# Quarter loads of the expert weights, output weights two units ahead in two buffers, and half of the single slots' second product in float32, in an attention, mixture-of-experts and gated-unit kernel

## The chip, the cores and the metric

The kernel runs as one program on 1 core of one Trainium2 chip. The metric is device time in microseconds (us). The engines are named as the profile names them: PE (TensorE, matmuls; PEld is its weight load), DVE (VectorE), ACT (ScalarE), POOL (GpSimd) and SP (SyncE, which here only issues DMAs). L12 is line 12 of the kernel before; the changed kernel has line numbers of its own.

## The reference

Three layers follow one another on 4608 tokens of width 512.

```python
kv = np.einsum('bhsd,bhse->bhde', k, v)          # 8 batches, 8 heads, 576 tokens, head size 64
out = np.einsum('bhsd,bhde->bhse', q, kv)
rms = np.sqrt(np.mean(out * out, axis=-1, keepdims=True) + 1e-06)
x = out / rms * g_norm                           # then as (4608, 512)

logits = x @ w_gate + modality_bias[modality_id] # 8 experts, one is chosen per token
e_idx = np.argmax(logits, axis=1)
gate_w = softmax(logits)[e_idx]
y[mask] = gate_w[mask] * (np.maximum(x[mask] @ w1[e], 0.0) @ w2[e])   # w1 512x1024, w2 1024x512

gate = 1.0 / (1.0 + np.exp(-(y @ w_gate)))       # the gated unit: w_gate, w_val 512x1536, w_out 1536x512
out = gate * (y @ w_val) @ w_out
```

## The kernel before, in words

**Attention and routing** fill the first 155 us or so: the keys' and values' products, the queries' turns and products in float32 (L296), then the ranks of the tokens within their experts.

**The expert stage** walks through 22 items that are always there and 4 spare ones behind a branch. Items 0 to 17 are pairs (two tiles of 128 tokens of one expert), items 18 to 21 are single slots (one tile each). Item t has four steps, j = 0 to 3, each with 256 of the 1024 hidden columns. A step (loop in `run`) does: the first product into `ph` (`emit_B`), the nonlinearity (`emit_h`), the second product of the step before into `py` (`emit_D`), and for single slots a turn of the hidden tile through PE (`emit_T`, tiles `hs`, `htp`). Products are split: each float32 operand is cut into a rounded part and a rest (`w1h`, `w1l` and so on, `split_w`, L738 on ACT and L739 on DVE), and three matmuls in float32r stand for one in float32.

The raw weights of item t lie in `w1r[t % 2]` and `w2r[t % 2]`, two buffers of 2 MiB for each matrix. (Buffer 0 of both is the tile `half` in the trace.) The kernel loads them two items ahead, a whole matrix per DMA, on SP (`load_w`, L699): w1 of item t+2 at step j = 2 of item t, w2 at j = 3, when the last quarter of the old contents has been split. The load is conditional: if the expert is that of item t, nothing is moved.

**Beside the expert stage** the weights of the gated unit, stored as doubles, are turned into float32 (`Decode`), and in the last four items the first rows of the expert output are read back, weighted and turned (`later`, `flip0`). A first unit's products (`gv_first`) follow the last step, then the last `emit_D` and `emit_y`, then every engine loads the count of used slots (L962) and branches (L963) round the spare items.

**The gated stage** has 60 units s, five blocks of 12; block 0 has units 0 to 11. In block 0 a unit is `glu_plain`: 12 matmuls of 128x512 for the gate product, 12 for the value product, and `out_step`: 12 for the output product of the unit before (L1109 to L1111). Between the products `prepare(s, spot)` is called at spots 0, 1, 6, 7, 2, 5, 4, 3, in this order. It sets the order of each engine's work: at spot 0 SP loads the next rows of weights, the next raw double weights and, in units 2 to 5, two `yr` tiles of the next block; spot 6 loads the output weights `wo` of the next unit into one buffer (`load_raw`, L554); spot 5 has POOL fetch gate values by index (`number`), spot 2 weights `yr` with them on ACT (`weigh`), spot 4 makes `wos`, `gh`, `gl` ready for the next output product (`ready_o`, L1088 to L1094) and turns `yr` on PE (L578); spot 3 decodes one late unit of weights and stores it (`decode_late2`, L148 to L152 and L1149 to L1159). SP takes all its DMAs in program order, and each instruction there that has to wait holds what is behind it.

In later blocks a unit is `glu_unit`, seven products of 6 matmuls and two output products. `YPLAN` says at which unit and spot which sum or split of the next block's inputs is made on ACT and DVE.

Of the kernel before, what the change touches and what calls it, by code (L numbers as in the profile page):

```python
# [82 lines left out]
def attention_moe_glu_kernel(  # L83
# [466 lines left out]
    raw_o = {}  # L550
# [127 lines left out]
    with ExitStack() as st:  # L678
# [9 lines left out]
        def load_w(t, which):  # L688
            if t >= end:
                return  # L690
            if which == 0:
                regs[t] = (nc.sync.value_load(est[0:1, t:t + 1], min_val=0, max_val=E - 1),
                           nc.sync.value_load(est[0:1, NITEM + t:NITEM + t + 1], min_val=0, max_val=1) if t < NSURE else None)
            if t >= NSURE:
                return
            e, new = regs[t]
            src, dst = (w1, w1r) if which == 0 else (w2, w2r)
            src = src[bass.ds(e, 1), :, :].rearrange("o (c p) f -> p (o c) f", p=128)
            nc.sync.dma_start(out=dst[t % 2], in_=src, cond=new, cond_hint=False)  # L699

        def load_piece(t, j, which):
            e = regs[t][0]
            p = dec.tile([128, 1024], F32, tag="d_raw", name="d_raw", bufs=4)
            if which == 0:
                src = w1[bass.ds(e, 1), :, j * 256:j * 256 + 256]
            else:
                src = w2[bass.ds(e, 1), j * 256:j * 256 + 256, :]
            p = p.rearrange("p (c f) -> p c f", f=src.shape[2])
            nc.sync.dma_start(out=p, in_=src.rearrange("o (c p) f -> p (o c) f", p=128))
            return p  # L710
# [12 lines left out]

        def split_w(t, j, which):
# [3 lines left out]
            raw, dst = ((w1r, w1s), (w2r, w2s))[which]  # L728
            nm = f"w{which + 1}"
            shape = [128, KC, 256] if which == 0 else [128, 2, DM]  # L730
            if t >= NSURE:
                src = load_piece(t, j, which)
            elif which == 0:
                src = raw[t % 2][:, :, j * 256:j * 256 + 256]
            else:
                src = raw[t % 2][:, 2 * j:2 * j + 2, :]
# [58 lines left out]
        def emit_T(t, j):  # L795
# [11 lines left out]
        def emit_D(t, j):  # L807
# [92 lines left out]
        def gv_first():  # L900
# [3 lines left out]
            glu_plain(lambda k: wt_first[k // 2][:, k % 2], y_of0, bank, tmp, lambda h: gm0, lambda p: None)  # L904

        def run(lo, hi):
# [10 lines left out]
            for which in range(2):  # L917
                for t in range(lo, lo + ahead):
                    load_w(t, which)
# [6 lines left out]
            for s, (t, j) in enumerate(steps):  # L926
# [5 lines left out]
                nt, nj = steps[s + 1] if s + 1 < len(steps) else (end, 0)  # L932
                split_w(nt, nj, 0)
# [21 lines left out]
            if sure:  # L955
                gv_first()
            emit_D(*steps[-1])
            emit_y(hi - 1)

        end = 0  # L960
        run(0, NSURE)
        used = nc.values_load(est[0:1, 2 * NITEM:2 * NITEM + 1], min_val=0, max_val=NSLOT)  # L962
        with tc.If(used > NSURE + NPAIR):  # L963
# [4 lines left out]
    with ExitStack() as st:  # L968
# [21 lines left out]
        gms = {(0, 0): gm0}  # L990
        split_o, split_g, acc = {}, {}, {}
# [279 lines left out]
```

## Time and profile before

| | |
|---|---|
| median of 3 runs | 1556.83 us (1555.05 to 1560.03) |
| the profiled execution | 1559.3 us |
| its span, first to last instruction | 1557.5 us |
| mean granted PE clock | 0.968 of full |
| PE busy | 1452.1 us (93%) |
| DVE, ACT, POOL busy | 919.9, 644.6, 229.3 us |
| mean DMA rate over the span | 229 GB/s |

The span lies 1.8 us below the profiled execution's own time. Busy shares are averages over stages that differ: the attention's first 155 us, the expert stage to about 660 us, block 0 of the gated stage to about 807 us, and the later blocks. PEclk of 1.00 is the clock of 2.4 GHz, 0.5 would be 1.2 GHz throughout.

### The profile page before, as it was taken

To read this page: it belongs to the slowest core of one execution; us is meant where nothing else is said; L and a number is where in the kernel's file an instruction comes from. 1 tells how busy PE (TensorE), PEld (TensorE's weight loads), DVE (VectorE), ACT (ScalarE), POOL (GpSimd) and SP (SyncE) were. 2 spreads that over 40 slices of the span, in tenths; PEclk is the share of its full clock that TensorE was granted. 3 is DMA by queue.
4 is the path that set the end of the run, shared out by engine and by line. 5 is a ranking of instruction groups with operands and counts; after the bars stand their busy time and mean duration, and the time that the engine had idled before them with its cause. 6 is when DMAs were issued, how large, how long until landed. Compare 5 with 4: busy or idle time off the path is not lost.

```text
span 1557.5 us, 22220 instructions
## 1 busy us (share of the span) xinstructions
PE 1452.1 (93%) x8649; PEld 1242.1 (80%) x8649; DVE 919.9 (59%) x1416; ACT 644.6 (41%) x1011; POOL 229.3 (15%) x302
## 2 busy tenths in 40 slices
PE   6993899999999998877789999999999999999997
PEld 5983799999999997655578887888888888888886
DVE  2568687887887886634576667434463346534341
ACT  3656455555555556723333334222232233212121
POOL 1121221232232122002001100102010020101011
PEclk9997899999999999988899999999999999999999
DMA  9976877857875747557578664656465655555444
GB/s 297 318 263 245 217 248 272 293 176 273 294 274 186 273 154 275 191 178 251 192 258 297 248 243 188 243 191 246 173 225 200 237 197 216 201 198 208 191 165 152
DMA packets 121950, 356.24 MB, mean 229 GB/s; under 512 B 18289, under 2 KB 39025, under 8 KB 114673
## 3 DMA queue, kind: packets, MB, share of 16 engines
q1 hardware_dynamic: 107632, 318.16, 57.7%
q0 software_dynamic: 11488, 36.27, 6.5%
q8 instruction: 70, 1.15, 0.3%
q10 hardware_dynamic: 2720, 0.35, 0.2%
q14 instruction: 40, 0.32, 0.1%
HBM read 311.27 MB, written 68.63 MB: 244 GB/s over the span
## 4 chain that ended last, share of the span: by engine, by line
PE 82%; issue 5%; DMA 5%; DVE 4%; ACT 2%; POOL 1%; SPq 0%; POOLq 0%; another core or an unknown queue 0%; ACTq 0%; DVEq 0%
PE gv L641 10%; PE gv L643 10%; PE gv L642 10%; PE ac L1109 6%; PE ac L1111 6%; PE ac L1110 6%; PE py L817 5%; PE py L816 5%; PE py L818 5%; PE ph L779 4%; PE ph L778 4%; PE ph L777 4%; PE kv L259 2%; PE ops L296 2%; DMA wo<-w_d 1%
## 5 line engine op out<-in xcount | busy, mean ns | idle before, releaser
L1109 PE MATMUL ac<-wos,gh 128*128 128x512 f32 x432 | 175.6, 406 | 28.0 <-ACT gh L1093 28.0
L1111 PE MATMUL ac<-wos,gl 128*128 128x512 f32 x432 | 175.1, 405 | 0.2
L1110 PE MATMUL ac<-wos,gh 128*128 128x512 f32 x432 | 174.3, 403 | 0.0
L645 DVE TENSOR_TENSOR gm<-u,gv 128x512 f32<-128x512 f32 x96 | 65.9, 686 | 173.9 <-PE gv L643 172.9
L777 PE MATMUL ph<-xh,w1h 128*128 128x256 f32 x576 | 166.8, 290 | 0.8 <-ACT xh L760 0.8
L779 PE MATMUL ph<-xl,w1h 128*128 128x256 f32 x576 | 164.0, 285 | 0.0
L778 PE MATMUL ph<-xh,w1l 128*128 128x256 f32 x576 | 163.8, 284 | 0.0
L665 ACT ACTIVATE s<-gv 128x512 f32<-128x512 f32 x48 | 28.8, 600 | 264.5 <-issue 207.6
L816 PE MATMUL py<-w2h,hh 128*128 128x512 f32 x320 | 126.6, 396 | 4.6 <-ACT hh L803 4.4
L817 PE MATMUL py<-w2l,hh 128*128 128x512 f32 x320 | 126.6, 396 | 0.8 <-DVE w2l L739 0.8
L818 PE MATMUL py<-w2h,hl 128*128 128x512 f32 x320 | 125.4, 392 | 0.0
L1109 PEld LDWEIGHTS ac<-wos,gh 128*128 128x128 f32 x432 | 84.6, 196 | 49.3 <-ACT gh L1093 32.1
L641 PE MATMUL gv<-half,wt 128*128 128x512 f32 x288 | 113.3, 394 | 1.9 <-DMA wt<-wt_d 1.9
L777 PEld LDWEIGHTS ph<-xh,w1h 128*128 128x128 f32 x576 | 111.2, 193 | 2.5 <-ACT xh L760 1.2
L643 PE MATMUL gv<-half,wt 128*128 128x512 f32 x288 | 112.4, 390 | 0.0
L778 PEld LDWEIGHTS ph<-xh,w1l 128*128 128x128 f32 x576 | 111.4, 193 | 1.4
L642 PE MATMUL gv<-half,wt 128*128 128x512 f32 x288 | 112.1, 389 | 0.0
L779 PEld LDWEIGHTS ph<-xl,w1h 128*128 128x128 f32 x576 | 111.1, 193 | 0.3 <-DVE xl L761 0.3
L1120 POOL DMA_INDIRECT out_dram<-ot,to x36 | 37.2, 1034 | 463.7 <-DVE ot L1115 191.8
L645 DVE TENSOR_TENSOR s<-u,gv 128x512 f32<-128x512 f32 x48 | 33.0, 687 | 119.7 <-PE gv L643 119.7
L1111 PEld LDWEIGHTS ac<-wos,gl 128*128 128x128 f32 x432 | 84.7, 196 | 21.6 <-DVE gl L1094 3.3
L1110 PEld LDWEIGHTS ac<-wos,gh 128*128 128x128 f32 x432 | 84.5, 196 | 18.2
(268 smaller groups left out, 3341.8 us busy)
## 6 DMA issues: line engine op xcount, KB each, us to landing
wt<-wt_d SPq DMA_DIRECT2D x36, 1792.0 KB, 7.5
half<-in_moe_w_dram SPq DMA_DIRECT2D x24, 2048.0 KB, 9.4
wos<-wo_d SPq DMA_DIRECT2D x96, 512.0 KB, 8.2
w1r<-in_moe_w_dram SPq DMA_DIRECT2D x11, 2048.0 KB, 9.2
w2r<-in_moe_w_dram SPq DMA_DIRECT2D x11, 2048.0 KB, 10.9
rows<-w_d SPq DMA_DIRECT2D x24, 512.0 KB, 7.3
wt_d<-wt SPq DMA_DIRECT2D x12, 1024.0 KB, 5.2
kt<-in_k_dram SPq DMA_DIRECT2D x8, 1152.0 KB, 8.9
```

Source lines behind the costliest of these rows:

```text
L641: nc.tensor.matmul(out=o, lhsT=wh, rhs=yh[:, c, :], start=first and c == 0, stop=False, skip_group_check=True)
L642: nc.tensor.matmul(out=o, lhsT=wh, rhs=yl[:, c, :], start=False, stop=False, skip_group_check=True)
L643: nc.tensor.matmul(out=o, lhsT=wl, rhs=yh[:, c, :], start=False, stop=last and c == 1, skip_group_check=True)
L777: nc.tensor.matmul(out=o, lhsT=bh[:, c, cs], rhs=hi[:, c, 0:n], start=(c == 0), stop=False)
L778: nc.tensor.matmul(out=o, lhsT=bl[:, c, cs], rhs=hi[:, c, 0:n], start=False, stop=False)
L779: nc.tensor.matmul(out=o, lhsT=bh[:, c, cs], rhs=lo[:, c, 0:n], start=False, stop=(c == KC - 1))
L816: nc.tensor.matmul(out=o, lhsT=hi[:, f, cs], rhs=bh[:, f, :], start=first, stop=False)
L817: nc.tensor.matmul(out=o, lhsT=hi[:, f, cs], rhs=bl[:, f, :], start=False, stop=False)
L818: nc.tensor.matmul(out=o, lhsT=lo[:, f, cs], rhs=bh[:, f, :], start=False, stop=last)
L1109: nc.tensor.matmul(out=o, lhsT=gh[:, cs], rhs=wh, start=(k == 0), stop=False)
L1110: nc.tensor.matmul(out=o, lhsT=gh[:, cs], rhs=wl, start=False, stop=False)
L1111: nc.tensor.matmul(out=o, lhsT=gl[:, cs], rhs=wh, start=False, stop=(k == NJ - 1))
```

## The change

Six edits.

1. `load_w` loads a quarter of a matrix (512 KiB) instead of a whole one, still on SP and conditional, for each step: the quarter of w1 of item t+2 as soon as the same quarter of item t has been split, the quarter of w2 likewise. A w1 quarter is read in rows of 1 KB, where the whole matrix had rows of 4 KB; w2 rows are 2 KB as before. `read_item` reads an item's expert and condition.
2. In single slots the second product of steps j = 1 and 3 is made in float32 from the raw weights and the unsplit hidden tile (`plain`): no split of w2 there (L738, L739), no rest of the hidden tile, and one matmul in place of three. The w2 quarter's load then waits for that product.
3. `gv_first` takes the last `emit_D` and `emit_y` between its two products, and the count is loaded ahead of it, so the branch follows the value product.
4. `wo` has a second buffer in the gated stage's pool; `load_raw` moves from spot 6 of unit s, for unit s+1, to spot 0 of unit s, for unit s+2, ahead of the rows.
5. `load_wt` loads in two pieces, the first of which holds the weights of the first product. Some tiles of the gated stage are named early, which places them elsewhere in memory.
6. `YPLAN` for blocks from 1 on spreads the steps over other spots.

```diff
     def load_raw(s, k):
-        raw_o[s, 0] = y0p.tile([128, DM], F32, tag="wo", name="wo", bufs=1)
+        raw_o[s, 0] = (y0p if k % 2 == 0 else late_pool[0]).tile([128, DM], F32, tag="wo", name="wo", bufs=1)
...
-            nc.sync.dma_start(out=dst[t % 2], in_=src, cond=new, cond_hint=False)
...
+        def load_w(t, j, which):
+            if t < min(end, NSURE):
+                e, new = regs[t]
+                nc.sync.dma_start(out=part(t, j, which), in_=source(e, j, which), cond=new, cond_hint=False)
...
+        def plain(t, j, which=1):
+            return t >= NPAIR and which == 1 and j % 2 == 1
...
+            if plain(t, j, which):
+                dst[t, j] = (src, None)
+                return
...
+            if plain(t, j):
+                h = ws.tile([128, 256], F32, tag="hs", name="hs").rearrange("p (f k) -> p f k", f=2)
+                nc.scalar.activation(out=h, in_=ps, func=ACTF.Copy)
+                hT_t[t, j] = (h, None)
+                return
...
+                    if lo is None:
+                        nc.tensor.matmul(out=o, lhsT=hi[:, f, cs], rhs=bh[:, f, :], start=first, stop=last)
+                        continue
...
                 split_w(nt, nj, 0)
-                if j == NJ1 - 2:
-                    load_w(t + ahead, 0)
+                if nj == 0:
+                    read_item(nt + ahead)
+                load_w(nt + ahead, nj, 0)
                 emit_h(t, j)
                 split_w(t, j, 1)
-                if j == NJ1 - 1:
-                    load_w(t + ahead, 1)
+                if not plain(t, j):
+                    load_w(t + ahead, j, 1)
...
                     emit_D(*steps[s - 1])
+                    if plain(*steps[s - 1]):
+                        load_w(steps[s - 1][0] + ahead, steps[s - 1][1], 1)
...
+            count.append(nc.values_load(est[0:1, 2 * NITEM:2 * NITEM + 1], min_val=0, max_val=NSLOT))
+            gv_first(last)
...
-                 {(10, 1): "cd", (10, 7): "ea", (10, 4): "f", (11, 1): "i", (11, 6): "g", (11, 7): "k", (11, 5): "bj", (11, 2): "h"}]
+                 {(10, 5): "c", (10, 2): "d", (10, 4): "e", (10, 3): "af", (11, 7): "i", (11, 5): "g", (11, 2): "k", (11, 4): "b", (11, 3): "jh"}]
...
-                nc.sync.dma_start(out=wts[s % 2][:, 0:n].bitcast(F32), in_=wt_d[s % NJ][:, 0:n])
+                for lo, hi in ((0, 1), (1, n)):
+                    nc.sync.dma_start(out=wts[s % 2][:, lo:hi].bitcast(F32), in_=wt_d[s % NJ][:, lo:hi])
...
             if spot == 0:
                 load_wt(s + 1)
+                if s + 2 <= NJ:
+                    load_raw(s + 2, s + 1)
                 load_rows(s + 2)
```

SP in one unit of block 0, before. `w_d<-w2r` is the store of the decoded weights, `rows` the next weight rows, `w2r<-in_moe_w` the next raw double weights, `wo` the output weights of the next unit:

```order
L150 DMA w_d_74<-w2r_8538 512x1x128
L1037 DMA rows_2065<-w_d_73 128x1024
L1144 DMA w2r_8538<-in_moe_w_out_dram 128x1024
L1129 DMA yr<-y_d 128x528 x2
L554 DMA wo<-w_d_73 128x512
L1062 DMA wt_d_80<-wt_7631 128x1536
L1090 DMA wo_d_91<-wos 128x1024
```

The same unit in the changed kernel:

```order
L150 DMA w_d_74<-w2r_8517 512x1x128
L554 DMA wo<-w_d_73 128x512
L1069 DMA rows_2065<-w_d_73 128x1024
L1175 DMA w2r_8517<-in_moe_w_out_dram 128x1024
L1160 DMA yr<-y_d 128x528 x2
L1095 DMA wt_d_80<-wt_7697 128x1536
L1121 DMA wo_d_91<-wos 128x1024
```

The `wo` load stands four issues earlier, and it is now the load for the unit after the next one; the store of the decoded weights is still ahead of all loads.

SP in the single slots, before, around the loads for item 20 (`half` is buffer 0):

```order
L699 DMA half_1706<-in_moe_w_dram 128x4x1024
L894 DMA rows_2065<-w_d_72 128x1024
L894 DMA rows_2066<-w_d_72 128x1024
L699 ISA
L699 DMA half_1706<-in_moe_w_dram 128x8x512
```

In the changed kernel quarters for item 20 stand even ahead of the first read of the expert output (`d_raw<-y_d`), and the rest is spread over the steps:

```order
L708 DMA half_1706<-in_moe_w_dram 128x4x256
L708 ISA
L708 DMA half_1706<-in_moe_w_dram 128x2x512
L880 DMA d_raw<-y_d 128x512
L881 DMA oid<-y_d 128x1
```

What was two DMAs of 2 MiB has become eight of 512 KiB; the first quarter of each matrix is issued three steps earlier than the whole was.

PE at the end of the expert stage, before: the value product of `gv_first` (`xtp`), the last second product (`py`), the count and the branch:

```order
L616 MATMUL xtp<-half_7565,d_raw 128x512
L617 MATMUL xtp<-half_7565,d_raw 128x512
L816 MATMUL py_7603<-w2h,hh 128x512
L817 MATMUL py_7603<-w2l,hh 128x512
L818 MATMUL py_7603<-w2h,hl 128x512
L816 MATMUL py_7603<-w2h,hh 128x512
L817 MATMUL py_7603<-w2l,hh 128x512
L818 MATMUL py_7603<-w2h,hl 128x512
L962 TENSOR_LOAD est
L963 COMPARE_AND_BRANCH
```

In the changed kernel, from the end of the gate product (`ph`) to the value product's first rows:

```order
L616 MATMUL ph<-half_7637,d_raw 128x512
L617 MATMUL ph<-half_7637,d_raw 128x512
L828 MATMUL py_7671<-w2r_2072,hs 128x512 x2
L615 MATMUL xtp<-half_7637,d_raw 128x512
L616 MATMUL xtp<-half_7637,d_raw 128x512
```

The last second product, two float32 matmuls on the raw weights in place of six, now lies between the two products; the count stands ahead of both, and the branch behind the value product.

## Rows read from the trace of the kernel before

**Rows 1.** Stretches of 40 us: engine busy us (instructions), granted clock, DMA share, GB/s

```profile
200.00:240.00 40.00, 40.00 (x261) 36.45 (x260) 31.64 (x39) 22.53 (x30) 7.75 (x9) 1.00 0.80 272
...
600.00:640.00 40.00, 31.86 (x181) 26.74 (x179) 27.48 (x32) 28.56 (x47) 9.11 (x10) 0.91 0.85 310
...
720.00:760.00 40.00, 31.70 (x116) 24.51 (x117) 19.91 (x31) 16.98 (x30) 4.98 (x8) 0.83 0.57 199
...
920.00:960.00 40.00, 37.47 (x159) 30.15 (x158) 30.55 (x45) 16.33 (x25) 0.00 (x0) 0.96 0.52 195
```

**Rows 2.** Waits from 655 to 812 us: engine line <- released by: total us, times, longest

```profile
ACT wos L1088 <- DMA wo<-w_d: 74.0, 10, 9.4
...
PE ac L1109 <- ACT gh L1093: 28.0, 9, 5.9
```

**Rows 3.** The chain that ended last, 700 to 815 us: start, us, what

```profile
742.81 0.32 SPq L152
...
744.67 5.99 DMA wo<-w_d
```

**Rows 4.** PE in order of time, in two units of the first block: start, us, what

```profile
736.68 0.50 PE L1109 MATMUL ac<-wos,gh 128*128 128x512 f32 x1 [2.29 <-ACT gh L1093]
...
744.30 1.03 PE L578 MATMUL tr<-ident,yr 128*128 128x128 f32 x8
...
751.94 0.60 PE L1109 MATMUL ac<-wos,gh 128*128 128x512 f32 x1 [3.85 <-ACT gh L1093]
```

**Rows 5.** PE at the end of the single slots, the branch, the first block's start

```profile
652.75 0.38 PE L801 MATMUL htp<-ident,hs 128*128 128x128 f32 x2
...
662.05 0.47 PE L615 MATMUL gv<-half,wt 128*128 128x512 f32 x1 [2.02 <-PEq L963]
...
669.14 0.50 PE L1109 MATMUL ac<-wos,gh 128*128 128x512 f32 x1 [2.83 <-ACT gh L1093]
...
673.93 0.39 PE L615 MATMUL gv<-half,wt 128*128 128x512 f32 x1
...
676.66 0.39 PE L615 MATMUL gv<-half,wt 128*128 128x512 f32 x1
```

**Rows 6.** DMA from 700 to 760 us, all queues together

```profile
DMA packets 5287, 13.18 MB, mean 220 GB/s; under 512 B 673, under 2 KB 1704, under 8 KB 5284
```

**Rows 7.** As rows 1, a stretch at the start of the second block

```profile
800.00:840.00 40.00, 38.06 (x168) 31.14 (x168) 29.87 (x52) 14.85 (x26) 7.48 (x11) 1.00 0.91 331
```

**Rows 8.** SyncE's DMA issues from 719 to 752 us

```profile
728.49 0.87 SPq L1129 DMA_DIRECT2D yr<-y_d  x2
```

**Rows 9.** POOL, the same stretch

```profile
734.13 0.18 POOL L566 COPY oid<-yr 128x1 int32<-128x1 int32 x1 [11.82 <-DMA yr<-y_d]
```

**Rows 10.** PE in order of time, 590 to 610 us, in the single slots

```profile
591.57 0.38 PE L801 MATMUL htp<-ident,hs 128*128 128x128 f32 x2
...
595.06 0.38 PE L801 MATMUL htp<-ident,hs 128*128 128x128 f32 x2
...
598.19 0.38 PE L801 MATMUL htp<-ident,hs 128*128 128x128 f32 x2
```

**Rows 11.** PE later in the single slots

```profile
625.61 0.56 PE L816 MATMUL py<-w2h,hh 128*128 128x512 f32 x1 [4.37 <-ACT hh L803]
...
640.75 0.66 PE L578 MATMUL xtp<-ident,d_raw 128*128 128x128 f32 x4 [1.03 <-DVE hl L804]
```

**Rows 12.** The chain that ended last, 598 to 700 us

```profile
606.15 17.57 DMA half<-in_moe_w_dram
```

**Rows 13.** The chain that ended last, 0 to 60 us, float32 matmuls of the attention

```profile
31.46 0.98 PE ops L296 x8
```

**Rows 14.** ACT at the branch

```profile
667.94 0.63 ACT L1088 ACTIVATE wos<-wo 128x512 fp32r<-128x512 f32 x1 [7.23 <-DMA y_d<-y,sidx]
```

**Rows 15.** PE at the start of the second block

```profile
806.93 0.50 PE L641 MATMUL gv<-half,wt 128*128 128x512 f32 x1 [1.94 <-DMA wt<-wt_d]
```

**Rows 16.** PE late in the second block

```profile
942.52 0.50 PE L641 MATMUL gv<-w2r,wt 128*128 128x512 f32 x1 [2.14 <-DVE u L645]
```

More of the change, by code (lines that the diff above doesn't have):

```diff
@@ L686, in attention_moe_glu_kernel, with read_item, part, source @@
         NJ1 = F1 // 256
[L688 to L691, printed above, removed]
+        def read_item(t):
+            if t < end:
                 regs[t] = (nc.sync.value_load(est[0:1, t:t + 1], min_val=0, max_val=E - 1),
                            nc.sync.value_load(est[0:1, NITEM + t:NITEM + t + 1], min_val=0, max_val=1) if t < NSURE else None)
[L694 to L698, printed above, removed]
-            nc.sync.dma_start(out=dst[t % 2], in_=src, cond=new, cond_hint=False)
-        def load_piece(t, j, which):
-            e = regs[t][0]
-            p = dec.tile([128, 1024], F32, tag="d_raw", name="d_raw", bufs=4)
+        def part(t, j, which):
+            if which == 0:
+                return w1r[t % 2][:, :, j * 256:j * 256 + 256]
+            return w2r[t % 2][:, 2 * j:2 * j + 2, :]
+        def source(e, j, which):
             if which == 0:
@@ L707, in load_piece @@
                 src = w2[bass.ds(e, 1), j * 256:j * 256 + 256, :]
+            return src.rearrange("o (c p) f -> p (o c) f", p=128)
+        def load_w(t, j, which):
+            if t < min(end, NSURE):
+                e, new = regs[t]
+                nc.sync.dma_start(out=part(t, j, which), in_=source(e, j, which), cond=new, cond_hint=False)
+        def load_piece(t, j, which):
+            p = dec.tile([128, 1024], F32, tag="d_raw", name="d_raw", bufs=4)
+            src = source(regs[t][0], j, which)
             p = p.rearrange("p (c f) -> p c f", f=src.shape[2])
-            nc.sync.dma_start(out=p, in_=src.rearrange("o (c p) f -> p (o c) f", p=128))
+            nc.sync.dma_start(out=p, in_=src)
             return p
@@ L727, in split_w @@
                 return
-            raw, dst = ((w1r, w1s), (w2r, w2s))[which]
+            dst = (w1s, w2s)[which]
             nm = f"w{which + 1}"
             shape = [128, KC, 256] if which == 0 else [128, 2, DM]
[L731 to L736, printed above, removed]
+            src = load_piece(t, j, which) if t >= NSURE else part(t, j, which)
+            if plain(t, j, which):
+                dst[t, j] = (src, None)
+                return
             hi, lo = ((w1p, ws)[which].tile(shape, F32R, tag=nm + z, name=nm + z, bufs=3) for z in "hl")
@@ L916, in run @@
                 nc.gpsimd.dma_start(out=w2r[1], in_=w2[0].rearrange("(c p) f -> p c f", p=128))
-            for which in range(2):
-                for t in range(lo, lo + ahead):
-                    load_w(t, which)
+            for t in range(lo, lo + ahead):
+                read_item(t)
+                for which in range(2):
+                    for j in range(NJ1):
+                        load_w(t, j, which)
             split_w(lo, 0, 0)
@@ L932, in run @@
                 nt, nj = steps[s + 1] if s + 1 < len(steps) else (end, 0)
+                if s == 0:
+                    read_item(t + ahead)
+                    load_w(t + ahead, j, 0)
                 split_w(nt, nj, 0)
-                if j == NJ1 - 2:
-                    load_w(t + ahead, 0)
+                if nj == 0:
+                    read_item(nt + ahead)
+                load_w(nt + ahead, nj, 0)
                 emit_h(t, j)
                 split_w(t, j, 1)
-                if j == NJ1 - 1:
-                    load_w(t + ahead, 1)
+                if not plain(t, j):
+                    load_w(t + ahead, j, 1)
                 if not s and sure:
@@ L954, in run, with last @@
                     decode(s, "exponent", "words", "finish", "store")
[L955 to L960, printed above, removed]
+            def last(p=7):
+                if p == 7:
+                    emit_D(*steps[-1])
+                    emit_y(hi - 1)
+            if not sure:
+                last()
+                return
+            count.append(nc.values_load(est[0:1, 2 * NITEM:2 * NITEM + 1], min_val=0, max_val=NSLOT))
+            gv_first(last)
+        end, count = 0, []
         run(0, NSURE)
-        used = nc.values_load(est[0:1, 2 * NITEM:2 * NITEM + 1], min_val=0, max_val=NSLOT)
-        with tc.If(used > NSURE + NPAIR):
+        with tc.If(count[0] > NSURE + NPAIR):
             run(NSURE, NITEM)
@@ L990, in attention_moe_glu_kernel @@
         gms = {(0, 0): gm0}
+        for t in ("s1", "u3", "s2", "u2"):
+            ws.tile([128, HC], F32, tag=t, name=t, bufs=2 if t == "u2" else 1)
+        ws.tile([128, 4, 256], F32, tag="wsum", name="wsum", bufs=1)
+        for t in ("gh", "gl"):
+            ws.tile([128, HC], F32R, tag=t, name=t)
         split_o, split_g, acc = {}, {}, {}
```

12 lines of the change are left out of this document (6 added, 6 removed).

## The prediction

> **What bounds the kernel now.** I read the 40 us stretches first, then the waits, then the chain and each engine's work in order of time where PE is not full. The pairs are PE-bound: from 200 to 240 us PE is busy 40.00 of 40 us at the full clock, with DMA at 0.80 of its share. Three stretches are not: the single slots (31.86 us busy), block 0 of the gated stage (31.70 us at a mean clock of 0.83, while DVE is busy 19.91, ACT 16.98 and DMA 0.57, so none of them is full), and a place late in block 1 (37.47 us, 0.96) [rows 1]. The kernel can only gain where PE waits or runs at the lower clock, so these three are worked out; the other stretches are left as they are.
>
> In block 0 the waits name one cause: ACT waits 74.0 us, ten times, for `wo`, and PE 28.0 us for `gh`, which ACT makes right after [rows 2]. The chain shows why `wo` is late: SP stores a decoded unit (L152) at 742.81 and issues `wo` only at 744.67, behind the store and other loads; it lands 5.99 us later [rows 3]. Then `wos`, `gh`, the decoding on ACT and DVE and the store follow, and the store holds the next `wo`. That is a ring: one turn is the distance of two output products, 751.94 - 736.68 = 15.3 us [rows 4].
>
> **Block 0.** From the branch to the first product of block 1 it takes 806.93 - 662.05 = 144.9 us for units 1 to 11 [rows 5, 15]. PE's own work: 12 matmuls take 676.66 - 673.93 = 2.73 us at the full clock [rows 5], a unit has 36, so 8.2 us; units 3 to 6 add the turns of `yr`, 1.03 us [rows 4]. Sum 11 x 8.2 + 4 x 1.03 = 94.3 us, the lower bound. The change issues `wo` at spot 0 of the unit before the one that needs it, into the other buffer. It still stands behind the decoded store, but has a whole unit to land, so ACT no longer waits for it, and the decoding starts when `gh` is made, not when `wo` lands: the ring is cut.
>
> What is late next is DMA. Block 0 moves 220 GB/s [rows 6], with 15.3 us per unit 3.4 MB for a unit that has all its transfers (2 to 6, roughly; the later ones have no `yr`, then no raw doubles). The change moves the same bytes. At the start of block 1 the trace sustains 331 GB/s, DMA share 0.91, with PE busy 38.06 of 40 us [rows 7]: 3.4 MB take 10.2 us at that rate. That adds 1.0 us to each of units 3 to 6 and 2.0 us to unit 2: 6 us. I add 1.5 us for the lower clock after the branch and 2 us for small waits. Block 0 becomes 94.3 + 6 + 1.5 + 2 = 104 us, a gain of 41. Bounds: 50.6 (PE alone) and 19 (rival A).
>
> The first unit after the branch is inside these 144.9 us: from 662.05 to 673.93 PE does 24 matmuls, 5.5 us of work, in 11.9 us [rows 5], because `gh` was late.
>
> **Single slots.** From the second turn of `hs` at 591.57 [rows 10] to the last at 652.75 [rows 5] are 14 steps in 61.2 us. An undisturbed step takes 598.19 - 595.06 = 3.13 us, one with a turn of four tiles more 595.06 - 591.57 = 3.49, so 0.36 us per such turn [rows 10]. There are seven (three of the items' inputs, four of `flip0`): 14 x 3.13 + 7 x 0.36 = 46.3 us. The other 14.9 us are waits and the lower clock after them: PE waits 4.37 us at 625.61 through `hh`, and 1.03 us at 640.75 for DVE [rows 11]. The first has its origin in the load: w2 of item 20 is issued at 606.15 and takes 17.57 us [rows 12], since it could start only when item 18 had used the whole old matrix.
>
> With quarters each load starts eight steps, some 25 us, ahead of its use. Items 20 and 21 need 8.4 MB; with the read-back rows, weight rows and stores about 12 MB fall into the first 25 us of the stage, 36 us at 331 GB/s [rows 7]; so the queue falls back by up to 11 us, less than the 25 us of lead. The load waits go.
>
> The float32 product costs PE something. No row shows a 128x512 one. The nearest is the attention's, four matmuls of 144 columns (two records each) in 0.98 us [rows 13]: 0.245 us each, 1.70 ns per column, 0.87 us for 512 columns, against three float32r ones at 2.73 / 12 = 0.23 us, 0.68 together. A plain step has two: +0.38 us, seven such steps between the two turns, +2.7 us. Bounds 0 (as three) and 5.4 (twice that). In exchange ACT and DVE lose a split in every other step; DVE is busy 27.48 of 40 us there [rows 1], so I count that only as cover. The 1.03 us wait lies at a step with j = 0, where the split stays; I keep it. Sum 46.3 + 2.7 + 1.0 = 50.0 us, gain 11.2, with bounds 6 (half of the waits stay) and 14.
>
> **The branch.** PE's gap of 2.02 us there comes from its own branch [rows 5] and stays, since the branch still follows the last matmul; the earlier count hides at most a part. The last second product becomes 0.4 us longer: -0.4. ACT stood still 7.23 us until 667.94 for the store of `y` [rows 14]; that store is now issued before the value product, some 2.7 us earlier in PE's order, and the moved tiles take the wait off `wos`. Its worth is inside block 0's sum.
>
> **Smaller ones.** The wait of 1.94 us for `wt` before block 1 [rows 15] lies inside the 144.9 us and goes with the first small piece. In block 1 PE waits 2.14 us for a DVE sum at 942.52, where `YPLAN` puts two steps on one spot [rows 16]; the stretch loses 40 - 37.47 = 2.5 us and 0.04 x 40 = 1.6 us of clock [rows 1]. The steps are the same and only spread: I take 3 of 4.1, bounds 0 and 4.1. The two halves of `load_wt` and the quarter loads cost SP issues: two issues take 0.87 us [rows 8], so six more per item are 2.6 us of an item that keeps PE busy over 20 us: hidden behind the pairs' matmuls, as nothing there waits for SP. If that cover were gone they would cost rival B.
>
> **Sum.** 41 + 11.2 - 0.4 + 3 = 54.8 us. The profiled execution took 1559.3 us (span 1557.5), so it would take 1504.5; it stands 2.5 us above the median of 1556.8, and against that the forecast is 1502 us. Its own range is a gain of 40 to 66, 1491 to 1517.
>
> **Rivals.** A: the ring is cut at `wo` but another one holds the units. `yr` is issued behind the same store and its fetch on POOL starts only at 734.13, 4.8 us after the issue ended [rows 8, 9], then come two fetches, the weighting on ACT and PE's turns. ACT takes these in order ahead of `wos` and `gh`. For it: POOL waited 11.82 us there. Against: the path has two units of time, and only units 2 to 5 load `yr`. If it held units 2 to 6 at 12.5 us and the other six at 10.5, block 0 took 126 us, gain 19, and the total 1524 us. Chance 0.12.
>
> B, on the other side: the quarter loads cost more DMA time per byte, and the pairs become DMA-bound. Their DMA share is 0.80 at 272 GB/s [rows 1]; it is full when a byte costs 1.25 times as much, and the pairs, about 430 us, then stretch with it. At 1.41 times, the loss of 55 us eats the gain; at 1.5 times it is 86 us, 1588 us. For it: w1 comes in rows of 1 KB, a quarter of those before. Against: block 1 moves transfers of 512 KiB to 1 MiB at 331 / 0.91 = 364 GB/s of full share, more than the pairs' 272 / 0.80 = 340 with whole matrices [rows 1, 7]. Chance 0.04. The Trainium skill has a rule that speaks for this rival, in DMA: Bandwidth & Descriptors, section on bandwidth: batch DMAs to 1 MiB or more for three quarters of the peak. By it the old loads of 2 MiB are right and the new ones of 0.5 MiB are too small; the trace does not agree, since rows 7 hold their rate with such transfers, several at once in flight.
>
> C: the loads in the single slots are still late, because the same 12 MB crowd the same time, or the float32 products cost twice what I take. Then this term is about 0 and the time 1513. For it: DMA share 0.85 in that stretch [rows 1]. Against: the 25 us of lead. Chance 0.06.
>
> **How the numbers follow.** The forecast has 0.78, A 0.12, B 0.04, C 0.06. The predicted time is the forecast's, 1502. The range of 8 in 10 goes from 1489, near the bounds' best sum (a gain of 68), to 1520, which takes in C and stops short of A and B. What a measurement of this kernel can tell from no change is about 0.3%, 4.7 us. Forecast, A and C are all faster by more; B lies on the other side, but its weaker degrees would end near zero: faster 0.95, same 0.02, slower 0.03.
>
> **What the profile of the changed kernel would show.** Right: no wait of ACT for `wo` in block 0, output products 8.5 to 10.5 us apart, DMA share near 0.9 from unit 2 to 6; no wait of ACT for `half` and w1 or w2 buffers in the single slots, their 14 steps in about 50 us, and float32 matmuls of about 0.87 us each; the pairs at PE busy 40 of 40. Wrong: output products still 12 us or more apart, with ACT waiting for `gate_t` or PE for `yr` (A); DMA share 1.0 and PE gaps between 200 and 560 us (B); the same load waits in the single slots (C).

## The result, and the profile after

The changed kernel takes 1511.03 us (median of 4 runs, 1509.02 to 1517.72) against 1555.94 us (4 runs, 1554.21 to 1560.03): ratio 0.9715, 95% interval 0.9678 to 0.9753. It is faster by 45 us; 1502 was forecast, with a range of 1489 to 1520.

The two profiled executions differ by 50.0 us (spans 1557.5 and 1507.5). Cut at the same instructions of PE, the 50.0 us fall on these stretches:

| stretch on PE | before | after | gain | forecast |
|---|---|---|---|---|
| start to the first `ph` of the pairs | 162.67 | 163.27 | -0.6 | 0 |
| to the second turn of `hs` in the single slots | 428.90 | 427.73 | 1.2 | 0 |
| 14 single steps, to the last turn of `hs` | 61.18 | 51.74 | 9.4 | 11.2 |
| to the first product behind the branch | 9.30 | 7.83 | 1.5 | -0.4 |
| block 0 | 144.88 | 110.10 | 34.8 | 41 |
| first product of block 1 to the end | 750.57 | 746.88 | 3.7 | 3 |

The first two rows are no effect of the change that could be told: over all variants below these stretches vary from 159.8 to 168.2 and from 427.4 to 431.9 us. The stretches of 40 us of the changed kernel, to be read against [rows 1, 7]; the columns are the same (busy us of PE, PEld, DVE, ACT and POOL, granted clock, DMA share, GB/s):

```profile
200.00:240.00 40.00, 40.00 (x261) 36.42 (x260) 33.38 (x42) 22.22 (x30) 10.96 (x10) 1.00 0.94 316
600.00:640.00 40.00, 37.91 (x222) 28.96 (x220) 28.63 (x33) 31.32 (x54) 11.20 (x12) 1.00 0.77 270
...
680.00:720.00 40.00, 34.13 (x145) 27.78 (x146) 20.79 (x34) 22.19 (x39) 8.50 (x13) 0.84 0.83 291
720.00:760.00 40.00, 40.00 (x174) 32.99 (x173) 32.33 (x49) 18.05 (x30) 0.00 (x0) 0.97 0.73 260
...
880.00:920.00 40.00, 39.36 (x175) 31.89 (x174) 32.38 (x44) 17.59 (x26) 0.00 (x0) 1.00 0.60 217
```

The pairs are as full as before, the single slots nearly so, and the place late in block 1 too. One stretch is still far from full: 680 to 720 us, inside block 0, with a clock of 0.84. What waits there is told by the waits of block 0, which answer to [rows 2] (engine line <- released by: total us, times, longest):

```profile
ACT yr L573 <- DMA gate_t<-gate_d,oid: 16.7, 5, 8.1
...
PE tr L578 <- ACT yr L573: 10.4, 4, 5.2
...
ACT s L621 <- DMA y_d<-y,sidx: 2.4, 1, 2.4
```

ACT's 74.0 us for `wo` and PE's 28.0 us for `gh` are gone from the list. In their place stand 16.7 us of ACT for `gate_t`, the gate values that POOL fetches for the rows `yr`, and 10.4 us of PE for the rows that ACT weights with them. PE in order of time shows that only two of the eleven units are held; the first row of each of six output products and PE's waits between them answer to [rows 4]:

```profile
661.74 0.39 PE L1140 MATMUL ac<-wos,gh 128*128 128x512 f32 x1
669.90 0.39 PE L1140 MATMUL ac<-wos,gh 128*128 128x512 f32 x1
680.70 1.12 PE L578 MATMUL tr<-ident,yr 128*128 128x128 f32 x4 [5.20 <-ACT yr L573]
682.77 1.11 PE L578 MATMUL tr<-ident,yr 128*128 128x128 f32 x4 [0.95 <-ACT yr L573]
688.38 0.40 PE L1140 MATMUL ac<-wos,gh 128*128 128x512 f32 x1
697.48 0.39 PE L1140 MATMUL ac<-wos,gh 128*128 128x512 f32 x1
706.54 0.39 PE L1140 MATMUL ac<-wos,gh 128*128 128x512 f32 x1
713.29 0.66 PE L578 MATMUL tr<-ident,yr 128*128 128x128 f32 x4 [1.15 <-ACT yr L573]
717.01 1.11 PE L578 MATMUL tr<-ident,yr 128*128 128x128 f32 x4 [3.06 <-ACT yr L573]
722.58 0.39 PE L1140 MATMUL ac<-wos,gh 128*128 128x512 f32 x1
```

The distances are 8.16 us without turns, just PE's own work, 9.1 with turns, but 18.5 and 16.0 us in units 3 and 6. Three of the four turns take 1.1 us, where the one at 713.29, behind a wait of 1.15 us, takes 0.66: PE works at the lower of its two clock levels (1.2 GHz) for a while after the longer waits, and the mean of 0.84 says for how long in sum: 2 x 0.16 x 40 = 12.8 of the 40 us from 680 to 720.

The path behind the first of these waits, on four engines, answers to [rows 8, 9]. SyncE's issues of unit 2:

```profile
664.72 0.56 SPq L150 DMA_DIRECT2D w_d<-w2r  x1
665.33 0.61 SPq L554 DMA_DIRECT2D wo<-w_d  x1
666.00 0.44 SPq L1069 DMA_DIRECT2D rows<-w_d  x1
666.54 0.39 SPq L1175 DMA_DIRECT2D w2r<-in_moe_w_val_dram  x1
667.04 1.06 SPq L1160 DMA_DIRECT2D yr<-y_d  x2
```

POOL, when the first `yr` has landed, and the fetch that it starts:

```profile
673.48 0.19 POOL L566 COPY oid<-yr 128x1 int32<-128x1 int32 x1 [23.44 <-DMA yr<-y_d]
674.22 1.00 POOL L569 DMA_INDIRECT gate_t<-gate_d,oid  x1 [0.55 <-POOL oid L566]
```

ACT, which waits for that fetch:

```profile
679.93 0.72 ACT L573 ACTIVATE yr<-yr,gate_t 128x512 f32<-128x512 f32 x1 [8.13 <-DMA gate_t<-gate_d,oid]
```

`yr` stands last in its unit, behind the decoded store, `wo`, `rows` and the raw doubles, and lands 6.4 us after its issue. The fetch of 128 gate values takes 5.7 us from issue to use; the DMA engines are full meanwhile (share 1.05, 372 GB/s from 674 to 680 us), while in the kernel before seven of the eight such fetches landed in 2.2 to 3.7 us. From the issue of `yr` to the start of the weighting it is 12.9 us, 13.6 with the weighting itself, and PE's units are now 8.2 us long. PE began unit 2 at 659.02 and was ready for the first turn at 675.50 (680.70 - 5.20), two units later; SyncE issued `yr` only 8.0 us into them, after 3.2 us of waiting for the decoding that the store needs.

### The profile page after: what moved, and what is told of

Same layout as the page of the kernel before. It is cut to its first block, busy times and chain, and to the rows that moved or that the text cites. A ratio compares the mean times of both kernels' runs of the same rounds, so it can differ in the third digit from the quotient of the medians.

```text
span 1507.5 us, 22902 instructions
## 1 busy us (share of the span) xinstructions
PE 1435.2 (95%) x8633; PEld 1229.7 (82%) x8633; DVE 908.7 (60%) x1400; ACT 638.5 (42%) x1003; POOL 228.0 (15%) x302
## 2 busy tenths in 40 slices
DMA packets 154980, 356.31 MB, mean 236 GB/s; under 512 B 20593, under 2 KB 74097, under 8 KB 147697
## 4 chain that ended last, share of the span: by engine, by line
PE 51%; DMA 0%; issue 0%; POOL 0%; DVE 0%; ACT 0%; POOLq 0%; ACTq 0%
PE gv L641 10%; PE gv L643 10%; PE gv L642 10%; PE ac L1142 6%; PE ac L1140 6%; PE ac L1141 6%; PE tr L578 1%; PE gv L615 1%; PE gv L617 1%; PE gv L616 1%; DMA gate_t<-gate_d,oid 0%; POOL out_dram L1151 0%; DVE u L645 0%; POOLq L1302 0%; ACT yr L573 0%
## 5 line engine op out<-in xcount | busy, mean ns | idle before, releaser
L1140 PE MATMUL ac<-wos,gh 128*128 128x512 f32 x432 | 168.6, 390 | 0.0
L1142 PE MATMUL ac<-wos,gl 128*128 128x512 f32 x432 | 168.5, 390 | 0.0
L1141 PE MATMUL ac<-wos,gh 128*128 128x512 f32 x432 | 168.1, 389 | 0.0
L831 PE MATMUL py<-w2l,hh 128*128 128x512 f32 x304 | 119.3, 393 | 0.0
L830 PE MATMUL py<-w2h,hh 128*128 128x512 f32 x304 | 119.3, 392 | 0.0
L832 PE MATMUL py<-w2h,hl 128*128 128x512 f32 x304 | 118.4, 389 | 0.0
L1142 PEld LDWEIGHTS ac<-wos,gl 128*128 128x128 f32 x432 | 81.1, 188 | 17.5
L1141 PEld LDWEIGHTS ac<-wos,gh 128*128 128x128 f32 x432 | 81.1, 188 | 17.3
L1140 PEld LDWEIGHTS ac<-wos,gh 128*128 128x128 f32 x432 | 81.1, 188 | 16.8
```

Source lines behind the costliest of these rows:

```text
L831: nc.tensor.matmul(out=o, lhsT=hi[:, f, cs], rhs=bl[:, f, :], start=False, stop=False)
L832: nc.tensor.matmul(out=o, lhsT=lo[:, f, cs], rhs=bh[:, f, :], start=False, stop=last)
L1140: nc.tensor.matmul(out=o, lhsT=gh[:, cs], rhs=wh, start=(k == 0), stop=False)
L1141: nc.tensor.matmul(out=o, lhsT=gh[:, cs], rhs=wl, start=False, stop=False)
L1142: nc.tensor.matmul(out=o, lhsT=gl[:, cs], rhs=wh, start=False, stop=(k == NJ - 1))
```

## Experiments

Ten variants ran, eight of them timed in three rounds beside the kernel before. Whole times of one variant scatter by 3 to 10 us; a part of it lies in the attention (the first `ph` starts between 159.8 and 168.2 us in these profiles), while the single slots and the stretch from block 1 on repeat within 0.3 us where nothing was changed in them, with one exception (747.67 instead of 746.88 us from block 1 on, in the first variant). Block 0, with its waits for `gate_t`, repeats within some 2 us (112.24 us in a variant that changes only a table used later). So each variant is read by its stretch first and by its time second. Ratios are to the kernel before. Rows of one engine give start, us, engine, line, operation, and the idle time before it with its releaser; line numbers shift between the variants, names are the same.

**Output weights one unit ahead again.**

```diff
-                if s + 2 <= NJ:
-                    load_raw(s + 2, s + 1)
...
-            if b:
+            if b == 0:
+                load_raw(s, k)
+            else:
```

> The changed kernel with one edit undone: output weights again one unit ahead, in one buffer, issued at spot 6 behind the unit's own output product. Theory (the ring of wo, half, gh, decoding and store was block 0's bound, and the second buffer two units ahead cuts it): the branch to block 1 goes from 110.1 us back to 140 to 147, ACT waits for wo again at most units, output products 13 to 16 us apart, total 1540 to 1548. Rival (the other edits at the branch, the early store of y and the moved tiles, gave much of it): block 0 at 120 to 130 us, total 1522 to 1532.

1541.06 us (1536.24 to 1543.66), ratio 0.9886 (0.9855 to 0.9916). Block 0 takes 142.49 us, and its waits are those of before:

```profile
ACT wos L1121 <- DMA wo<-w_d: 78.3, 9, 10.6
...
PE ac L1142 <- ACT gh L1126: 26.7, 8, 5.0
```

The ring was the bound; as long as it stands, the other edits take only 2.4 us off block 0.

**The output weights alone, on the kernel before.**

```diff
-        raw_o[s, 0] = y0p.tile(
+        raw_o[s, 0] = (y0p if k % 2 == 0 else late_pool[0]).tile(
...
                 load_wt(s + 1)
+                if s + 2 <= NJ:
+                    load_raw(s + 2, s + 1)
```

> The kernel before with one edit only: output weights issued two units ahead at spot 0, in two buffers, the second in the pool of the gated stage; all else, the old order of the tiles in that pool too, as before. Theory (this edit is nearly all of block 0's gain): block 0 at 108 to 120 us instead of 144.9, ACT's waits for wo gone after the first two units, the single slots' 14 steps still 60 to 62 us, total 1520 to 1532. Rival (without the early store of y and the moved tiles the first units wait at the branch, and the ring goes on): block 0 at 125 us or more, total over 1535.

1525.82 us (1522.23 to 1529.14), ratio 0.9804 (0.9777 to 0.9831). Block 0 takes 113.46 us, the 14 single steps 62.26 us. So this edit by itself is 31.4 of block 0's 34.8 us. The first output product starts 6.6 us behind the branch instead of 3.0; of these 3.6 us, the order of the tiles is 2.7 by the last variant below.

**yr ahead of the store.** The loads of `yr` in block 0 go to the last spot of the unit before; nothing else is moved.

```diff
-                if spot == 0:
+                if spot == 0 and b:
                     turn_at(j0, lambda i: load_y(b + 1, i))
+                if spot == 3 and b == 0:
+                    turn_at(j0 - 1, lambda i: load_y(b + 1, i))
```

> The changed kernel with the loads of yr in block 0 issued at the end of the unit before, ahead of the decoded store, wo, rows and the raw doubles of their own unit. Theory (rival A of the prediction holds two units, because yr lands late and the gate fetch behind it takes 5 us under load): POOL's 23.4 us wait for yr shrinks by about 5, PE's waits of 5.20 and 3.06 us for the weighting go, and the lower clock after them; block 0 at 97 to 103 us, total 1498 to 1505. Rival (the queues are full, what comes earlier makes wo or rows late by as much): PE waits the same time for other tiles, block 0 at 108 to 112 us, total 1508 to 1513.

1493.11 us (1491.08 to 1496.63), ratio 0.9584 (0.9557 to 0.9611): the fastest median of all, some 18 us below the changed kernel. The two profiled executions differ by 12.7 us, and the other 5 us lie within the scatter of whole times. Block 0 takes 97.06 us, 13.0 less. POOL has the first row 5.6 us earlier (its first copy here, to be read against the one above):

```profile
667.90 0.19 POOL L566 COPY oid<-yr 128x1 int32<-128x1 int32 x1 [17.56 <-DMA yr<-y_d]
```

The fetch itself is no quicker. In the same full DMA engines (share 1.01) it takes 7.1 us from its issue until ACT can use it; it only starts earlier:

```profile
668.64 1.39 POOL L569 DMA_INDIRECT gate_t<-gate_d,oid  x1 [0.55 <-POOL oid L566]
...
675.70 1.51 ACT L573 ACTIVATE yr<-yr,gate_t 128x512 f32<-128x512 f32 x2 [1.21 <-DMA gate_t<-gate_d,oid]
```

PE's waits for weighted rows shrink from 10.4 to 1.9 us in sum, in these four:

```profile
676.48 1.44 PE L578 MATMUL tr<-ident,yr 128*128 128x128 f32 x8 [0.48 <-ACT yr L573]
686.51 0.66 PE L578 MATMUL tr<-ident,yr 128*128 128x128 f32 x4 [0.37 <-ACT yr L573]
687.58 0.66 PE L578 MATMUL tr<-ident,yr 128*128 128x128 f32 x4 [0.41 <-ACT yr L573]
697.53 0.66 PE L578 MATMUL tr<-ident,yr 128*128 128x128 f32 x4 [0.61 <-ACT yr L573]
```

The stretches of block 0 in this variant:

```profile
680.00:720.00 40.00, 38.62 (x181) 31.42 (x180) 28.48 (x45) 24.16 (x41) 7.49 (x12) 1.00 0.89 323
720.00:760.00 40.00, 40.00 (x178) 33.10 (x178) 34.26 (x53) 18.55 (x30) 3.70 (x7) 1.00 0.89 323
```

The clock is full, and nothing else came late by as much: the rival falls. What the change lost in block 0, it lost to the issues that stand ahead of `yr`, the first of them the store that waits for the decoding.

**No float32 products.**

```diff
         def plain(t, j, which=1):
-            return t >= NPAIR and which == 1 and j % 2 == 1
+            return False
```

> The changed kernel with all second products of the single slots as three float32r ones, quarters kept. Theory (float32 costs PE 0.38 us a step, and ACT and DVE have room for the splits): from the second turn of hs to the last 49 us instead of 51.7, total 1507 to 1511. Rival (ACT and DVE are what the single slots wait for next, so seven more splits of each hold PE): 54 to 60 us there, total 1514 to 1520.

1506.3 us (1501.63 to 1511.18), ratio 0.9668 (0.963 to 0.9706). The 14 steps take 51.46 us instead of 51.74. Neither theory holds: PE's products are shorter, but its waits grow. With the float32 half they are these three, 1.96 us in sum:

```profile
615.47 0.39 PE L778 MATMUL ph<-w1l,xh 128*128 128x256 f32 x1 [0.43 <-DVE w1l L745]
619.15 0.44 PE L807 MATMUL htp<-ident,hs 128*128 128x128 f32 x2 [0.71 <-ACT hs L792]
...
631.62 0.66 PE L578 MATMUL xtp<-ident,d_raw 128*128 128x128 f32 x4 [0.82 <-DVE hl L815]
```

Without it they are five, 3.40 us:

```profile
619.25 0.39 PE L778 MATMUL ph<-w1l,xh 128*128 128x256 f32 x1 [0.44 <-DVE w1l L745]
622.92 0.44 PE L807 MATMUL htp<-ident,hs 128*128 128x128 f32 x2 [0.71 <-ACT hs L792]
635.12 0.66 PE L578 MATMUL xtp<-ident,d_raw 128*128 128x128 f32 x4 [1.03 <-DVE hl L815]
640.24 0.66 PE L578 MATMUL xtp<-ident,d_raw 128*128 128x128 f32 x4 [0.97 <-DVE hl L815]
644.31 0.39 PE L778 MATMUL ph<-w1l,xh 128*128 128x256 f32 x1 [0.25 <-DVE w1l L745]
```

Behind the last turn it saves 0.43 us more (7.40 against 7.83). Block 0 was 4.6 us shorter in this profile, mostly in unit 6 (11.6 us instead of 16.0); whether float32 has to do with that is asked again below.

**Whole matrices, no float32 products.** In that variant, the loads of a matrix are put together again.

```diff
-                load_w(nt + ahead, nj, 0)
+                if j == NJ1 - 2:
+                    load_all(t + ahead, 0)
...
-                    load_w(t + ahead, j, 1)
+                if j == NJ1 - 1:
+                    load_all(t + ahead, 1)
```

> The changed kernel with whole-matrix weight loads as before the change (w1 two steps and w2 one step ahead of the item's end) and no float32 products, since these read the raw weights a step longer. Theory (the quarters removed the late loads of the single slots): the same 14 steps take 59 to 62 us, PE waits of 3 to 5 us near the second step of item 20, and the waits for w2h and w2l near 171 us return (1.1 us); total 1517 to 1522, so 8 to 12 above the kernel with quarters and no float32 products. Rival (the loads come in time without the quarters, the gain came from the float32 half): 50 to 53 us there, total within 3 us of it.

1521.26 us (1514.25 to 1524.12), ratio 0.9781 (0.9755 to 0.9807). The 14 steps take 61.49 us, 10.0 more than with quarters, and 15 us more by the medians. PE waits at the places of before [rows 11] and through the same loads (ACT 4.1 us for w1 and 6.3 us for w2 of item 20); its two longest waits:

```profile
611.60 0.44 PE L814 MATMUL htp<-ident,hs 128*128 128x128 f32 x2 [2.98 <-ACT hs L799]
...
623.48 0.80 PE L837 MATMUL py<-w2h,hh 128*128 128x512 f32 x1 [4.76 <-ACT hh L821]
```

The small waits for the first w2, 0.24 and 0.82 us near 170 us, are back too. So the quarters are the whole gain of the single slots.

**yr early and no float32 products.** The two edits above together:

```diff
-            return t >= NPAIR and which == 1 and j % 2 == 1
+            return False
...
+                if spot == 3 and b == 0:
+                    turn_at(j0 - 1, lambda i: load_y(b + 1, i))
```

> The changed kernel with yr issued early as in the run above, and with no float32 products as in the run above. Theory (without float32 the singles and the branch are worth 0.7 us; the other 4.6 us that block 0 was shorter without float32 came from when the gate fetches landed, and this wait is gone with the early yr): block 0 96 to 98 us, total 1490 to 1494. Rival (float32 costs block 0 something of its own): block 0 at 92 to 94 us, total 1486 to 1489. If ACT, with the splits back, makes the weighting of yr late: 98 us or more.

1493.77 us (1490.36 to 1495.96), ratio 0.96 (0.9571 to 0.9629), the same as with yr early alone. The single steps take 51.47 us, the way to the branch 7.40, block 0 95.54 against 97.06. So the float32 half is worth nothing that a measurement can tell. As long as `yr` was late, unit 6 took 11.6 to 12.0 us in the three profiles without float32 products and 16.0 to 17.4 in four of the five with them (9.1 in the fifth, where other units waited). Eight profiles would fall like that by chance about one time in fourteen, so this may be chance; if it isn't, the reason stays open. With `yr` early the difference is 1.5 us.

**The branch as before.**

```diff
-            count.append(nc.values_load(est[0:1, 2 * NITEM:2 * NITEM + 1], min_val=0, max_val=NSLOT))
-            gv_first(last)
+            gv_first(lambda p: None)
+            emit_D(*steps[-1])
+            emit_y(hi - 1)
...
         run(0, NSURE)
+        count.append(nc.values_load(est[0:1, 2 * NITEM:2 * NITEM + 1], min_val=0, max_val=NSLOT))
```

> The changed kernel with the branch edit undone: the last second product and the store of y again behind the value product, and the count read behind them, right at the branch. Theory (reading the count ahead of the matmuls hides it; before the change the gap at the branch was 2.02 us, now about 0.3): the gap is 1.7 to 2.1 us again, the store of y starts some 2.5 us later, the way from the last turn of hs to the first product behind the branch takes 9.3 to 9.8 us instead of 7.8, block 0 within 3 us of 110.1; total 1511 to 1516. Rival (the gap went for another reason, the moved tiles or the earlier store): the gap stays under 0.6 us.

1508.95 us (1508.13 to 1511.5), ratio 0.9706 (0.968 to 0.9732). The way from the last turn to the first product behind the branch takes 8.82 us instead of 7.83, with this gap:

```profile
651.75 0.50 PE L615 MATMUL gv<-half,wt 128*128 128x512 f32 x1 [1.20 <-ACTq L985]
```

In the changed kernel no idle time is recorded there: the last product before the branch starts at 650.02, the first behind it at 650.57, 0.3 us more than the 0.23 at which such products follow one another. The gap is the edit's work, by 1.0 us; it is 1.20 here and in the variant with the output weights alone, and the 2.02 of before [rows 5] is the longest of the three. The variant undoes the early read of the count and the order of the last products together, so which of them closes the gap is not told apart. The whole time doesn't show it, since block 0 has waits of another kind that move with it (units 1 and 4 take 13.7 and 16.8 us, the sum is 109.06). Unit 1 is long because `y` is stored late again: ACT waits 8.90 us for that store, instead of 2.4, and what stands behind it on ACT comes late.

```profile
661.83 0.60 ACT L621 ACTIVATE s<-gv 128x512 f32<-128x512 f32 x1 [8.90 <-DMA y_d<-y,sidx]
```

So the early store takes 5.5 us off unit 1 (13.66 to 8.16), but the sum of block 0 doesn't show them: unit 3, held by `gate_t` in the changed kernel, takes 10.97 us here instead of 18.5.

**The old table of the block sums.**

```diff
-                 {(10, 5): "c", (10, 2): "d", (10, 4): "e", (10, 3): "af", ...
+                 {(10, 1): "cd", (10, 7): "ea", (10, 4): "f", ...
```

> The changed kernel with the old table of the block sums for blocks 1 and later (two steps on one spot at the start of unit 10). Theory (the prediction's 3 us): PE's waits for the DVE sum near the end of block 1, 2 us, and the lower clock after them return, and in later blocks smaller ones; from the first product of block 1 to the end 749 to 752 us instead of 746.8, total 1512 to 1515. Rival (the 3.7 us that this stretch gained came from the wt load's small piece or from variation): within 1 us of 746.8.

1508.67 us (1505.6 to 1512.98), ratio 0.9698 (0.9664 to 0.9732). From the first product of block 1 to the end it takes 748.88 us, 2.0 more than 746.88. The wait is the old one, to be read against [rows 16]:

```profile
896.49 0.50 PE L641 MATMUL gv<-w2r,wt 128*128 128x512 f32 x1 [2.14 <-DVE u L645]
```

The stretch around it in this variant (columns as in [rows 1]):

```profile
880.00:920.00 40.00, 37.47 (x166) 30.24 (x165) 31.92 (x44) 16.59 (x24) 0.00 (x0) 1.00 0.51 184
```

The variant with the output weights alone has the same table, the same wait of 2.14 us and the same 37.47 us busy, and yet needs 750.55 us for the stretch:

```profile
890.00:930.00 40.00, 37.47 (x159) 30.10 (x158) 30.70 (x45) 16.24 (x24) 0.00 (x0) 0.96 0.52 195
```

There the clock fell to its lower level after the wait (0.96 over 40 us: 1.6 us lost), in the variant with only the table it stayed at 1.00. Both mechanisms that the forecast added for this step are seen apart.

**Two small ones, one profile each.** Weight rows of later blocks in one piece again:

```diff
-                for lo, hi in ((0, 1), (1, n)):
+                for lo, hi in ((0, n),):
```

> The changed kernel with the weight rows of blocks 1 and later read in one piece a unit again. Theory (the small first piece took the wait off the start of block 1, and with the moved tiles and the table is the rest of what the stretch behind block 0 gained): PE waits 1 to 2.5 us for wt at the first product of block 1, and the stretch from there to the end is 1 to 2 us longer than 746.9. Rival (that wait went because the ring no longer delays the load): no wait of PE for wt, both stretches within 0.5 us.

1511.23 us. PE waits 1.2 us for `wt` at the first product of block 1, block 0 takes 111.10, the stretch behind it 747.03: the small piece is worth about 1 us. And the tiles of the gated stage in their old order:

```diff
-        for t in ("s1", "u3", "s2", "u2"):
-            ws.tile([128, HC], F32, tag=t, name=t, bufs=2 if t == "u2" else 1)
...
```

> The changed kernel with the tiles of the gated stage in their old order. Theory (in the old order wos takes the place of the y that is still being stored, so its first use waits for that store): ACT waits some 5 us for the store of y at the first or second wos instead of 2.4 at s, unit 1 starts its output product 2 to 4 us later, block 0 at 111 to 115 us, and the stretch behind it within 0.5 us of 746.9. Rival (the order of the tiles makes no difference once y is stored early): block 0 within 1.5 us of 110.1.

1514.09 us. ACT, before its first `wos`, waits for the store of `y`, as in [rows 14]:

```profile
657.48 0.63 ACT L1114 ACTIVATE wos<-wo 128x512 fp32r<-128x512 f32 x1 [6.76 <-DMA y_d<-y,sidx]
```

The first output product starts 5.7 us behind the branch instead of 3.0, and block 0 takes 112.45 us. So the new order is worth 2.7 us at the first unit: the store of `y` is waited for all the same, but only by `s`, for 2.4 us.

## Why the prediction came out as it did

The main step is shown: the ring of `wo`, `wos`, `gh`, decoding and store was block 0's bound, and loading two units ahead cuts it (142.49 with it, 110.10 without, 113.46 when it alone is cut). The total is 9 us above the forecast. Of these, 4.8 are the sum's (50.0 instead of 54.8, profile against profile); 2.5 were taken off because the profiled run of before lies above the median, and the profiled run of after lies 1.7 below its own.

**Block 0, 104 forecast, 110.1 measured: the step that failed is what is late next.** The forecast put 6 us there for DMA and gave rival A (the fetch of `gate_t` behind `yr`) a chance of 0.12, because its path has two units of time. It was the other way round. Rival A's mechanism holds two units, 10.4 us of waits and the lower clock after them, 13 us by the variant without them. It doesn't hold all of them, as that rival had it (126 us), so its time was wrong too. The two units of time of [rows 8, 9] were counted at the old unit length of 15 us; with units of 8.2 us they are 16.5 us, and 8.0 until the issue and 13.6 from there make 21.6. The path itself also grew, as the fetch takes 5.7 us instead of 2.2 to 3.7. DMA as a bound costs 2.8 us at most: with `yr` early the same bytes go through in 97.06 us, 2.8 above PE's 94.3, of which PE's waits for rows are 1.9. That 104 came within 6 us of the measured time is in part luck: the forecast had 9.5 us above PE's own work (6 for DMA, 3.5 for the clock and small waits) where 2.8 are needed once `yr` is early, and these 6.7 us too many cover half of the 13 that it left out. The 331 GB/s of [rows 7] was no ceiling: that variant moves more from 660 to 720 us, all queues together.

```profile
DMA packets 8445, 20.40 MB, mean 340 GB/s; under 512 B 997, under 2 KB 3045, under 8 KB 8440
```

At 340 GB/s a unit of 8.2 us has room for 2.8 MB. The forecast set 3.4 MB, 10.2 us, for each of units 2 to 6 against that. In that variant units 2 and 6 take 8.16 and 9.05 us, PE's own pace, and only units 3 to 5 come near it (10.15, 10.29 and 9.96 us); the one thing that PE waits for in its block 0 is weighted rows. That the fuller units borrow time from the emptier ones around them, since loads run two units ahead, is likely but not shown.

**Single slots, 50.0 forecast, 51.7 measured.** That the load waits go, by the quarters, is shown (61.49 against 51.46). The float32 product was sized right. Here are the two of one step (two records each) and the turn behind them:

```profile
628.27 1.88 PE L828 MATMUL py<-half,hs 128*128 128x512 f32 x4
629.99 0.38 PE L807 MATMUL htp<-ident,hs 128*128 128x128 f32 x2
```

From 628.27 to 629.99 are 1.72 us for two products, 0.86 each (forecast 0.87); a float32 step is 3.37 us instead of 3.05. Mis-sized was what remains of waits, 1.96 us instead of 1.0, and the turns of four tiles, taken at 0.36 us each: the step from 634.95 to 639.52 has two of them, in 1.20 us more than the 3.37 of a float32 step without. And the cover that the float32 half was said to be has a worth: seven such products cost 7 x 0.32 = 2.2 us, but the 14 steps are only 0.28 us longer with them (51.74 against 51.46), since 1.4 us of waits go and other steps come out shorter too.

**The branch, -0.4 forecast, +1.5 measured.** That the gap "stays, since the branch still follows the last matmul; the earlier count hides at most a part" failed. It follows the last matmul still, but the count is now read ahead of the value product, and with that edit, the moved last product included, 1.7 of the 2.02 us went. What the moved tiles and the early store would bring was left unsized inside block 0; by the variants without them it is 2.7 us at the first output product and 5.5 us in unit 1.

**Smaller ones, 3 forecast, 3.7 measured:** 2.0 us are the table's waits, 1.7 the clock after them, all within units 10 and 11 of block 1 and nothing behind them.

**Rival B is refuted.** The kernel moves the same bytes in smaller transfers (154980 packets instead of 121950), and PE stays at 40.00 of 40 in every stretch from 200 to 600 us. A full share would move 316 / 0.94 = 336 GB/s from 200 to 240 us, against 340 with whole matrices: 1% dearer per byte, where 25% would have been needed. The Trainium skill, in DMA: Bandwidth & Descriptors, section on bandwidth, asks for transfers of 1 MiB or more; at 0.5 MiB, several in flight, this trace shows no loss that matters, and the measurement decides. **Rival C** is refuted by the single slots: two waits of DVE, 0.2 us each, are all that is left there for a weight load, and the float32 product costs 0.86 us and not twice that. The crowd that it feared is there, as the DMA engines are full from 611 to 631 us (share 1.00, 364 GB/s), but the loads are issued early enough to stand it.

## What to carry to other kernels

When a ring that sets the length of a loop is cut, count the other paths' slack again in units of the new length: a path that takes 13 us from its issue had two units of time, enough at 15 us a unit, and was late at 8. Among loads issued at one place, the first should be the one with work of several engines behind it (here row, fetch, weighting, turn), not the one that is largest; moving that one line was worth 13 us here, and made the fastest kernel of this study, 1493.11 us. And read a small edit by the stretch that it touches: whole times of one variant scatter by 3 to 10 us, the undisturbed stretches mostly by 0.3.

## What the runs showed of the hardware

- The clock after a wait isn't a fixed price: after the same wait of 2.14 us with the same work around it, it fell in one variant (0.96 of 40 us) and stayed at 1.00 in another.
- A gap of 1.2 us (2.0 in one profile) stood before the first matmul behind a branch when the branch's operand was read right at it; read some 7 us of PE work earlier, with another product last before the branch, 0.3 us remained.
- A fetch of 128 values by index took 5.7 us, and 7.1 in another variant, until ACT could use them while the DMA engines were full (share 1.05 and 1.01); with the DMA at 0.68 of its share, in the kernel before, it landed in 2.2 to 3.7 us.
